# An mLSTM cell followed by a leaky-ReLU block: w_in in eight pieces, and the first chunk's mask and decay summed in PSUM

## The chip, the cores and the metric

The kernel runs on one core of a Trainium2 chip. The metric is the time of one execution on the device in microseconds. A core has TensorE (PE, matrix products into PSUM), VectorE (DVE), ScalarE (ACT), GpSimd (POOL) and SyncE (SP), which here issues DMAs. Each engine works through its own queue of instructions, and semaphores make one wait for another.

## The reference

Inputs are q, k, v and o_gate of shape (4, 8, 768, 40), two gates of shape (4, 8, 768), w_in (320, 2048) and w_out (2048, 320). Cut to what matters:

```python
for t in range(S):                       # S = 768, for each batch and head
    m_new = maximum(f[t] + m, i[t])
    fs, is_ = exp(f[t] + m - m_new), exp(i[t] - m_new)
    C = fs * C + is_ * outer(v[t], k[t])
    n = fs * n + is_ * k[t]
    den = maximum(abs(n @ q[t]), 1.0)
    y[t] = sigmoid(o[t]) * (C @ q[t]) / den
x = y as (B * S, H * D)                  # (3072, 320)
h = x @ w_in
out = maximum(0.01 * h, h) @ w_out       # (3072, 320)
```

The two weights arrive as 64-bit floats and are narrowed to 32 bits on the chip.

## The kernel before

The sequence is cut into six chunks of 128 positions. A "step" s is one chunk c and one batch b (s = 4c + b), with all eight heads. Within a chunk the recurrence is written as products: the decay between two positions is the exponential of a + bias, with a from scans along the sequence (`gates`, L193) and a triangular mask; the scores k.q are multiplied by it and then by v; the state C carries over what lies before the chunk.

For a step the units are these. `u_transpose` (L305) transposes k and q on PE into PSUM (tkq), and ACT copies them to SBUF (kqT, L314). `u_scores` (L316) makes the scores (sc, L323) and DVE multiplies the decay w by them (L327). `u_state` makes pc and dC (L337, L348), and in chunk 0 DVE copies dC into the state (L354). `u_values` multiplies w and v (pa, L367); in chunk 0 DVE copies pa to hn (L371) and makes den from it (L374 to L376). `gate` (L385, L388) makes x on DVE and POOL. `u_x` (L399 to L403) transposes x for the block that follows.

The decay w comes in two ways. From chunk 1 on, SP stores a in DRAM (L211) and reads it back spread over the partitions (`spread`, L255), POOL adds the mask (`prep_mask`, L279), and ACT takes the exponential (`prep_exp`, L287). In chunk 0, `spread_first` (L257) builds a spread over the partitions on PE (ab, L266), for two steps at a time, and DVE adds the mask (L273).

The feed-forward work of a chunk is `ff_units`. A first layer unit is, for chunk 0, a half: `half(j, h)` makes the features 2j and 2j + 1 for half h of the chunk's 512 rows (four products of L413 and two of L419, each of which is two instructions of 256 columns in the profile), and ACT applies the Prelu (L427). The second layer is `part(n, m)`, a quarter of the features for one block of 128 rows (L457), four parts to one output (L462).

Weights come in four pieces of w_in (four features each) and four of w_out. `load_weights(n)` issues the DMAs of piece n on SP into a raw 64-bit buffer, of which there are three. `narrow_weights(n)` (L154) is a generator that is called between other units: its first call queues the Abs on ACT (L166) and a first operation on DVE (L168), and each further call queues one more operation on DVE (L172, L176, L178, L180, L184). A piece may be used by PE after the sixth.

The order on PE, DVE, ACT and POOL is that of the code (a manual schedule); a scheduler orders SP. `first_chunk` (L503) writes out the order for chunk 0 by hand and puts in two halves, `ffs[0]` and `ffs[1]`, both from piece 0. The halves of a pair of j come together: (0, 1) for rows h = 0, then (0, 1) for h = 1, then (2, 3). The loop from L593 on takes the other thirty units of chunk 0's feed-forward work, with the cells of chunk 1 spread between them from unit 10 on; `todo` (L591) says at which unit the narrowing of a piece begins. Later chunks follow in the same way.

Of the kernel before, what the change touches and what calls it, by code (L numbers as in the profile page):

```python
# [9 lines left out]
F32 = mybir.dt.float32  # L10
# [8 lines left out]
def kernel(  # L19
# [90 lines left out]

    QN = NF // 4
    QC = 4 * P
    WC = KF * QC + 2 * P
    w_in = consts.tile([P, QN, WC], F32, name="w_in")
    w_out = consts.tile([P, NF, Dm], F32, name="w_out")

    def w_full(kk, f):
        n, e = divmod(f, 4)  # L120
        return w_in[:, n, kk * QC + e * P : kk * QC + (e + 1) * P]

    def w_rest(r, j):
        n, e = divmod(j, 2)
        return w_in[KR * r : KR * (r + 1), n, KF * QC + e * P : KF * QC + (e + 1) * P]

    wide = moe_w_in.dtype == U64
    raws = {}

    def load_weights(n):  # L130

        if n < QN:
            dst = w_in[:, n, :]
        else:
            dst = w_out[:, 4 * (n - QN) : 4 * (n - QN + 1), :].rearrange("p a d -> p (a d)")
        to = dst
        if wide:
            raw = wk.tile([P, dst.shape[1]], U64, name="raw", bufs=3)
            raws[n] = (raw, dst)
            to = raw[:]  # L140
        if n < QN:
            cols = slice(n * QC, (n + 1) * QC)
            for kk in range(KF):
                nc.sync.dma_start(to[:, ts(kk, QC)], moe_w_in[ts(kk, P), cols])
            rest = moe_w_in[KF * P :, cols].rearrange("d (j two e) -> two d j e", two=2, e=P)
            for r in range(2):
                nc.sync.dma_start(
                    to[KR * r : KR * (r + 1), KF * QC :].rearrange("p (j e) -> p j e", e=P), rest[r],
                )
        else:  # L150
            rows = moe_w_out[(n - QN) * QC : (n - QN + 1) * QC, :]
            nc.sync.dma_start(to.rearrange("p (a d) -> p a d", d=Dm), rows.rearrange("(a p) d -> p a d", p=P))

    def narrow_weights(n):  # L154
# [99 lines left out]
        d["w"] = wk.tile([P, H, P], F32, name="w", bufs=NL)  # L254
        nc.sync.dma_start(d["w"][:], a_dr[c, b * H : (b + 1) * H, :].partition_broadcast(P))  # L255

    def spread_first(a, s2):  # L257


        ab = [psf.tile([P, 2, H // RG, P], F32, name=f"ab{r}", tag="mm") for r in range(RG)]  # L260
        for n in range(2):
            for m in range(H // RG):
                for r in range(RG):
                    bh = (s2 + n) * H + m * RG + r
                    rows = ts(r, BH)
                    nc.tensor.matmul(  # L266
                        ab[r][:, n, m, :], lhsT=ident[rows, r * BH + bh : r * BH + bh + 1].to_broadcast([BH, P]),
                        rhs=a[rows, :], start=True, stop=True,
                    )
        for n in range(2):  # L270
            w = st[s2 + n]["w"] = wk.tile([P, H, P], F32, name="w", bufs=NL)
            for r in range(RG):
                nc.vector.tensor_tensor(  # L273
                    w[:, r::RG, :], ab[r][:, n], cmask[:].unsqueeze(1).to_broadcast([P, H // RG, P]), op=ALU.add,
                )

    def prep_mask(s):
        w = st[s]["w"]
# [2 lines left out]
    def prep_exp(s):  # L281

        c, b = divmod(s, B)
        w = st[s]["w"]
        for h in range(H):
            bh = b * H + h
            nc.scalar.activation(w[:, h, :], w[:, h, :], AF.Exp, bias=gT[:, c, 0, bh : bh + 1], scale=1.0)  # L287

    def prep_vu(s):

# [9 lines left out]
    def prep_o(s):  # L300

        nc.scalar.activation(st[s]["o"][:], st[s]["o"][:], AF.Tanh, scale=0.5)


    def u_transpose(s):  # L305
        d = st[s]
        d["kqT"] = wk.tile([P, 2, PR, P], F32, name="kqT")
        for i in range(2):
            tp = psc.tile([P, PR, P], F32, name="tkq", tag="c")
            for j in range(PR):  # L310
                nc.tensor.transpose(  # L311
                    tp[:, j, :], d["kq"][:, i, 2 * j : 2 * j + 2, :].rearrange("p h d -> p (h d)"), ident[:],
                )
            nc.scalar.copy(d["kqT"][:, i], tp[:])  # L314

    def u_scores(s):  # L316
        d = st[s]
# [11 lines left out]
    def u_state(s):  # L329
# [14 lines left out]
        if c + 1 < NB:  # L344
# [6 lines left out]
            for r in range(2):  # L351
                rows = slice(DP * r, DP * r + DP)
                if c == 0:
                    nc.vector.tensor_copy(C_new[rows, b, :, r, :], dC[rows])  # L354
                else:
                    g = gL[rows, c, b * H + r : (b + 1) * H : 2].unsqueeze(2).to_broadcast([DP, PR, D1])
                    nc.gpsimd.tensor_tensor(C_new[rows, b, :, r, :], C[rows, b, :, r, :], g, op=ALU.mult)
                    nc.vector.tensor_tensor(C_new[rows, b, :, r, :], C_new[rows, b, :, r, :], dC[rows], op=ALU.add)

    def u_values(s):  # L360
        c, b = divmod(s, B)
        d = st[s]
        hn = d["hn"] if c > 0 else wk.tile([P, H, D1], F32, name="hn")
        d["hn"] = hn
        pa = psc.tile([P, H, D1], F32, name="pa", tag="c")
        for h in range(H):
            nc.tensor.matmul(pa[:, h, :], lhsT=d["w"][:, h, :], rhs=d["va"][:, h, :], start=True, stop=True)  # L367
        if c > 0:
            nc.vector.tensor_tensor(hn[:], hn[:], pa[:], op=ALU.add)  # L369
        else:  # L370
            nc.vector.tensor_copy(hn[:], pa[:])  # L371

        den = d["den"] = wk.tile([P, H], F32, name="den")
        nc.vector.tensor_scalar(den[:], hn[:, :, D], scalar1=-2.0, scalar2=2.0, op0=ALU.mult, op1=ALU.max)  # L374
        nc.vector.scalar_tensor_tensor(den[:], in0=hn[:, :, D], scalar=2.0, in1=den[:], op0=ALU.mult, op1=ALU.max)
        nc.vector.reciprocal(den[:], den[:])  # L376
        if c > 0:
            gate(s)
# [28 lines left out]
    def ff_units(g):  # L407
# [56 lines left out]

        if g == 0:

            ins = [(j, h) for j0 in range(0, NF // 2, 2) for h in range(2) for j in (j0, j0 + 1)]
            return [lambda j=j, h=h: half(j, h) for j, h in ins] + [
                lambda n=n, m=m: part(n, m) for m in range(4) for n in range(B)
            ]  # L470
        return [u for j in range(NF // 2) for u in pair(j)] + [
# [26 lines left out]
    def feed(s):  # L498
        load(s)
        spread(s)  # L500
        load_o(s)

    def first_chunk():  # L503

        load(0)
        load(1)
        load_weights(0)
        load_o(0)
        load_o(1)
        load(2)  # L510
        load(3)
        load_weights(1)
        load_o(2)
        load_o(3)
        load_weights(2)
        load_weights(3)
        bu, a = gates(0)
        gates_T(0, bu)
        spread_first(a, 0)
        u_transpose(0)  # L520
        prep_exp(0)
        spread_first(a, 2)
        prep_vu(0)
        u_scores(0)
        u_state(0)
        prep_exp(1)
        u_transpose(1)
        prep_vu(1)
        bus[1] = gates(1)
        w = narrow_weights(0)  # L530
        next(w, None)
        next(w, None)
        u_values(0)
        prep_exp(2)
        u_scores(1)
        next(w, None)
        u_state(1)
        next(w, None)
        next(w, None)
        prep_o(0)  # L540
        u_values(1)
        gate(0)
        next(w, None)
        prep_o(1)
        gate(1)
        u_transpose(2)
        prep_vu(2)
        u_x(0)
        prep_exp(3)
        u_scores(2)  # L550
        u_x(1)
        u_state(2)
        ffs = ff_units(0)
        ffs[0]()
        u_transpose(3)
        prep_vu(3)
        w = narrow_weights(1)
        next(w, None)
        ffs[1]()
        next(w, None)  # L560
        prep_o(2)
        u_values(2)
        u_scores(3)
        gate(2)
        u_state(3)
        next(w, None)
        next(w, None)
        prep_o(3)
        u_values(3)
        gate(3)  # L570
        next(w, None)
        next(w, None)
        u_x(2)
        u_x(3)
        return ffs

    E = mybir.EngineType
    with tc.manual_schedule(engines={E.PE, E.DVE, E.Activation, E.Pool}):
        ffs = first_chunk()
        feed(B)  # L580
        load_weights(QN)
        load_weights(QN + 1)
        feed(B + 1)
        load_weights(QN + 2)
        load_weights(QN + 3)
        feed(B + 2)
        feed(B + 3)


        ffs = ffs[4:6] + ffs[2:4] + ffs[6:]  # L590
        todo = {0: 2, 4: 3, **{9 + 4 * n: QN + n for n in range(4)}}  # L591
        now = iter(())
        for c in range(1, NB + 1):  # L593
            if c > 1:
                ffs = ff_units(c - 1)
            cells = cell_units(c) if c < NB else []
            n_ff, n_c = len(ffs), len(cells)
            lead = 10 if c == 1 else 0
            done = 0
            for i in range(n_ff):  # L600
                if c == 1:
                    if i in todo:
                        for _ in now:
                            pass
                        now = narrow_weights(todo[i])
                    next(now, None)
                    next(now, None)
                    if i == 8:
                        u_gates(1)
                        ahead(B)  # L610
                if i == lead and c + 1 < NB:
                    bus[c + 1] = gates(c + 1)
                ffs[i]()
# [40 lines left out]
```

## Time and profile before

| | us |
|---|---|
| median of three runs | 622.41 (622.02 to 622.71) |
| the profiled execution | 623.18 |
| its span, first to last instruction | 621.0 |
| PE busy | 597.4 |
| PE idle by its timeline up to 165 us, the longest gaps | 5.5 (start), 2.9 at 30, 5.0 at 53, 1.7 at 93, 2.5 at 153 |
| four groups of DMA for one k, q or v tile, issue to landing | 3.1, 3.5, 2.8 (k, q, v) |
| w_in, 512 KB, issue to landing | 5.5 |

The page gives each engine's busy time, then the span in 40 slices of 15.5 us in tenths. In a timeline a line is start, duration, engine, source line, operation, operands and the number of instructions merged, and in brackets how long the engine had been idle and what ended that. In a table by stage the columns are the stage, its length, busy time of PE, of PE's weight loads, of DVE, ACT and POOL (with instructions), then the granted clock of TensorE, the busy share of the DMA engines and GB/s. Matrix products are pipelined: their rate is read from the distance between starts.

### The profile page before, as it was taken

What the parts mean: (1) busy time and instruction counts of PE and PEld (TensorE: products, weight loads), DVE (VectorE), ACT (ScalarE), POOL (GpSimd) and SP (SyncE); (2) the same over time, 40 slices, a digit from 0 to 9 for tenths busy, and PEclk for the clock granted to TensorE, in tenths of its full rate; (3) what the DMA queues carried; (4) which work ended last, traced back from release to release, by engine and by line L of the source; (5) the groups of instructions that cost most, each with busy time, mean ns of one, the idle gap of its engine ahead of it and who ended that gap; (6) DMA issues with size and microseconds to landing.
All of it is one profiled execution on the core that took longest, in us unless ns stands there. A gap on an engine that the chain in (4) does not pass through costs nothing.

```text
span 621.0 us, 7722 instructions
## 1 busy us (share of the span) xinstructions
PE 597.4 (96%) x3046; PEld 385.7 (62%) x3046; DVE 178.2 (29%) x343; ACT 185.7 (30%) x493; POOL 111.8 (18%) x110
## 2 busy tenths in 40 slices
PE   6986998998999999999999999999999999999997
PEld 5865666776554577654577745577745567743575
DVE  5838656886221121311121411211101111100000
ACT  4442345332334403144403144223043231012100
POOL 3023021554202220302202302202101010000000
PEclk9997999999899999999999999999999999999999
DMA  9999434433221331312321313303300000000000
GB/s 180 226 234 217 147 97 130 91 73 67 67 51 36 76 77 28 81 23 65 77 51 48 78 24 74 77 13 86 77 11 1 1 0 22 11 12 0 0 22 21
DMA packets 111346, 41.50 MB, mean 67 GB/s; under 512 B 101104, under 2 KB 105616, under 8 KB 111312
## 3 DMA queue, kind: packets, MB, share of 16 engines
q1 hardware_dynamic: 111024, 40.79, 29.0%
q8 instruction: 24, 0.39, 0.3%
q10 hardware_dynamic: 288, 0.23, 0.2%
q14 instruction: 10, 0.08, 0.0%
HBM read 37.00 MB, written 4.01 MB: 66 GB/s over the span
## 4 chain that ended last, share of the span: by engine, by line
PE 87%; DVE 5%; SPq 3%; POOL 1%; ACT 1%; issue 1%; DMA 1%; POOLq 0%; DVEq 0%; ACTq 0%
PE po L457 32%; PE ph L413 27%; PE ph L419 8%; PE pa L367 6%; PE sc L323 4%; PE pc L337 3%; PE tkq L311 3%; SPq L242 2%; PE dC L348 2%; POOL x L388 1%; PE xt L399 1%; DMA va<-in_v_dram 1%; DVE hn L369 1%; DVE x L385 1%; DVE w_in L176 0%
## 5 line engine op out<-in xcount | busy, mean ns | idle before, releaser
L457 PE MATMUL po<-w_out,act 128*128 128x320 f32 x768 | 221.4, 440 | 0.0
L413 PE MATMUL ph<-xT,w_in 128*128 128x512 f32 (+1 forms) x448 | 186.2, 552 | 0.4 <-DVE w_in L184 0.4
L457 PEld LDWEIGHTS po<-w_out,act 128*128 128x128 f32 x768 | 142.3, 191 | 55.0 <-issue 1.9
L413 PEld LDWEIGHTS ph<-xT,w_in 128*128 128x128 f32 x448 | 81.5, 195 | 68.8 <-issue 58.5
L427 ACT ACTIVATE act<-ph 128x512 f32<-128x512 f32 (+1 forms) x112 | 53.7, 531 | 151.6 <-PE ph L419 151.6
L388 POOL TENSOR_TENSOR x<-x,den 128x320 f32<-128x320 f32 x24 | 22.9, 955 | 396.6 <-DVE x L385 396.6
L327 DVE TENSOR_TENSOR w<-w,sc 128x512 f32<-128x512 f32 x48 | 30.7, 681 | 182.3 <-PE sc L323 182.3
L287 ACT ACTIVATE w<-w,gT 128x128 f32<-128x128 f32 x192 | 58.7, 397 | 13.0 <-POOL w L279 12.8
L419 PE MATMUL ph<-xT,w_in 64*128 64x512 f32 (+1 forms) x224 | 57.2, 588 | 0.0
L462 ACT COPY y<-po 128x320 f32<-128x320 f32 x24 | 10.2, 424 | 148.5 <-PE po L457 86.6
L367 PEld LDWEIGHTS pa<-va,w 128*128 128x128 f32 x384 | 49.1, 203 | 8.5 <-issue 5.9
L279 POOL TENSOR_TENSOR w<-w,cmask 128x1024 f32<-128x1024 f32 x20 | 50.1, 2503 | 0.0
L367 PE MATMUL pa<-va,w 128*128 128x41 f32 x384 | 49.5, 291 | 0.4 <-DVE w L327 0.4
L314 ACT COPY kqT<-tkq 128x512 f32<-128x512 f32 x48 | 26.1, 593 | 75.2 <-PE tkq L311 75.1
L419 PEld LDWEIGHTS ph<-xT,w_in 64*128 64x128 f32 x224 | 17.3, 189 | 36.3 <-issue 36.3
L323 PEld LDWEIGHTS sc<-kqT 40*128 40x128 f32 x384 | 26.1, 204 | 12.8 <-issue 5.3
L323 PE MATMUL sc<-kqT 40*128 40x128 f32 x384 | 30.4, 302 | 1.7 <-ACT kqT L314 1.7
L369 DVE TENSOR_TENSOR hn<-hn,pa 128x328 f32<-128x328 f32 x20 | 9.9, 496 | 74.9 <-PE pa L367 74.9
L311 PEld LDWEIGHTS tkq<-ident,kq 128*128 128x128 f32 x192 | 23.7, 152 | 10.8 <-issue 9.4
L311 PE MATMUL tkq<-ident,kq 128*128 128x128 f32 x192 | 28.3, 295 | 0.0
L341 DVE TENSOR_TENSOR hn<-pc,gT 128x328 f32<-128x328 f32 x20 | 10.0, 498 | 60.6 <-PE pc L337 60.6
L337 PEld LDWEIGHTS pc<-C,kqT 128*128 128x128 f32 x160 | 20.6, 191 | 7.0 <-issue 5.3
(65 smaller groups left out, 316.8 us busy)
## 6 DMA issues: line engine op xcount, KB each, us to landing
w<-a_dr SPq DMA_DIRECT2D x20, 512.0 KB, 4.9
raw<-in_moe_w_out_dram SPq DMA_DIRECT2D x4, 1280.0 KB, 5.7
raw<-in_moe_w_in_dram SPq DMA_DIRECT2D x8, 512.0 KB, 5.5
kq<-in_k_dram SPq DMA_DIRECT2D x24, 160.0 KB, 3.1
kq<-in_q_dram SPq DMA_DIRECT2D x24, 160.0 KB, 3.5
va<-in_v_dram SPq DMA_DIRECT2D x24, 160.0 KB, 2.8
o_sb<-in_o_gate_dram SPq DMA_DIRECT2D x24, 160.0 KB, 4.7
out_dram<-y SPq DMA_DIRECT2D x24, 160.0 KB, 1.8
```

Source lines behind the costliest of these rows:

```text
L279: nc.gpsimd.tensor_tensor(w[:], w[:], cmask[:].unsqueeze(1).to_broadcast([P, H, P]), op=ALU.add)
L287: nc.scalar.activation(w[:, h, :], w[:, h, :], AF.Exp, bias=gT[:, c, 0, bh : bh + 1], scale=1.0)
L311: nc.tensor.transpose(tp[:, j, :], d["kq"][:, i, 2 * j : 2 * j + 2, :].rearrange("p h d -> p (h d)"), ident[:],)
L323: nc.tensor.matmul(sc[r][:, j, :], lhsT=kqT[rows, 0, j, :], rhs=kqT[rows, 1, j, :], start=True, stop=True,)
L327: nc.vector.tensor_tensor(w[:, r::2, :], w[:, r::2, :], sc[r][:], op=ALU.mult)
L337: nc.tensor.matmul(pc[:, 2 * j : 2 * j + 2, :].rearrange("p h d -> p (h d)"), lhsT=d["kqT"][:, 1, j, :], rhs=C[:, b, j].rearrange("p h d - ...
L367: nc.tensor.matmul(pa[:, h, :], lhsT=d["w"][:, h, :], rhs=d["va"][:, h, :], start=True, stop=True)
L388: nc.gpsimd.tensor_tensor(x3, x3, d["den"][:].unsqueeze(2).to_broadcast([P, H, D]), op=ALU.mult)
L413: nc.tensor.matmul(ph[:, cols], lhsT=w_full(kk, f), rhs=xT[:, kk, cols], start=(kk == 0), stop=False,)
L419: nc.tensor.matmul(ph[r][:, cols], lhsT=w_rest(r, j), rhs=xT[KR * r : KR * (r + 1), KF, cols], start=False, stop=True,)
L427: nc.scalar.activation(acts[f][:, cols], ph[r][:, cols], AF.Prelu, alpha=0.01)
L457: nc.tensor.matmul(po[n][:], lhsT=acts[f][:, ts(n, P)], rhs=w_out[:, f, :], start=(f == 0), stop=(f == NF - 1),)
```

## The change

It does the following things.

- w_in is laid out in eight pieces of two features' columns each (640 columns in SBUF where there were 1280), and w_out is loaded in eight pieces too. Six raw buffers of half the size take the place of three.
- The halves of chunk 0 come as all eight j for rows h = 0, then all eight for h = 1. Half n of the first group uses piece n. `first_chunk` now holds all eight halves of the first group, with the narrowing of the eight pieces and the cells of steps 2 and 3 between them.
- In chunk 0 the mask is put into PSUM by a product of the identity and the mask (`mask_first`), and a is added by the products of `spread_first`, which no longer start a sum. The exponential on ACT reads PSUM. Steps 0 and 1 share four banks; steps 2 and 3 have two banks each and are made later, after `ffs[0]` and `ffs[2]`.
- For steps 0 and 1 DVE copies kqT; in chunk 0 ACT copies dC into the state, and hn is no longer copied: den and gate read pa in PSUM.
- `gates(1)` is called after `first_chunk`, and the loop for the remaining 24 units has the cells from unit 6 on and the narrowing of w_out, three operations to a unit, from unit 4 on.

The core of the diff:

```diff
-    QN = NF // 4
-    QC = 4 * P
+    NP = NF // 2
+    PC = 2 * P
...
-            raw = wk.tile([P, dst.shape[1]], U64, name="raw", bufs=3)
+            raw = wk.tile([P, dst.shape[1]], U64, name="raw", bufs=6)
...
+    def mask_first(steps, groups):
+        per = H // len(groups)
+        ab = {r: psf.tile([P, len(steps), per, P], F32, name=f"ab{r}", tag="mm") for r in groups}
+        for r in groups:
+            nc.tensor.matmul(
+                ab[r][:].rearrange("p n m t -> p (n m) t"), lhsT=ident[:],
+                rhs=cmask[:].unsqueeze(1).to_broadcast([P, len(steps) * per, P]), start=True, stop=False,
+                skip_group_check=True,
+            )
+        return ab
...
-                        rhs=a[rows, :], start=True, stop=True,
+                        rhs=a[rows, :], start=False, stop=True, skip_group_check=True,
...
-                nc.vector.tensor_tensor(
-                    w[:, r::RG, :], ab[r][:, n], cmask[:].unsqueeze(1).to_broadcast([P, H // RG, P]), op=ALU.add,
-                )
...
+            nc.scalar.activation(w[:, h, :], w[:, h, :] if c > 0 else st[s]["ab"][h], AF.Exp, bias=gT[:, c, 0, bh : bh + 1], scale=1.0)
...
+            if s < 2:
+                nc.vector.tensor_copy(d["kqT"][:, i], tp[:])
...
-                    nc.vector.tensor_copy(C_new[rows, b, :, r, :], dC[rows])
+                    nc.scalar.copy(C_new[rows, b, :, r, :], dC[rows])
...
-            ins = [(j, h) for j0 in range(0, NF // 2, 2) for h in range(2) for j in (j0, j0 + 1)]
-            return [lambda j=j, h=h: half(j, h) for j, h in ins] + [
+            return [lambda j=j, h=h: half(j, h) for h in range(2) for j in range(NP)] + [
...
+    narrowing = (x for n in range(2 * NP) for x in narrow_weights(n))
+    def narrow(count):
+        for _ in range(count):
+            next(narrowing, None)
...
+        ab = mask_first((0, 1), (0, 1, 2, 3))
         bu, a = gates(0)
         gates_T(0, bu)
+        spread_first(a, ab, (0, 1))
+        prep_exp(0)
         u_transpose(0)
...
+        narrow(3)
+        u_x(0)
+        u_x(1)
+        ffs = ff_units(0)
+        ffs[0]()
+        narrow(6)
+        ab = mask_first((2,), (0, 2))
+        spread_first(a, ab, (2,))
+        ffs[1]()
+        prep_exp(2)
+        narrow(6)
+        ffs[2]()
+        narrow(6)
+        ab = mask_first((3,), (0, 2))
+        spread_first(a, ab, (3,))
+        ffs[3]()
+        prep_exp(3)
+        narrow(6)
         u_transpose(2)
         prep_vu(2)
+        ffs[4]()
         u_scores(2)
+        narrow(3)
         u_state(2)
+        narrow(3)
+        u_values(2)
+        ffs[5]()
+        prep_o(2)
+        narrow(3)
+        gate(2)
         u_transpose(3)
         prep_vu(3)
+        narrow(3)
+        u_x(2)
         u_scores(3)
+        ffs[6]()
+        narrow(3)
         u_state(3)
+        u_values(3)
         prep_o(3)
         gate(3)
+        narrow(3)
+        ffs[7]()
         u_x(3)
-        return ffs
+        return ffs[8:]
...
+        bus[1] = gates(1)
...
-            lead = 10 if c == 1 else 0
+            lead = 6 if c == 1 else 0
...
+                if c == 1 and i >= 4:
+                    narrow(3)
+                if c == 1 and i == 5:
+                    u_gates(1)
+                    ahead(B)
```

## The prediction

> **What bounds the kernel now.** I read the page first, then the slices, then the table by stage, then the queues' timelines between 38 and 64 us.
>
> ```profile
> PE 597.4 (96%) x3046; PEld 385.7 (62%) x3046; DVE 178.2 (29%) x343; ACT 185.7 (30%) x493; POOL 111.8 (18%) x110
> PE   6986998998999999999999999999999999999997
> PEclk9997999999899999999999999999999999999999
> ```
>
> TensorE is busy 96%; the slices that are not full lie in the first sixth. Only there can a change of order gain or lose; from 165 us on PE is busy 451.8 of 456.0 us. The table by stage:
>
> ```profile
> 0.00:38.00 38.00, 29.40 (x227) 26.10 (x227) 25.30 (x60) 18.64 (x52) 8.97 (x20) 1.00 1.08 215
> 38.00:60.00 22.00, 16.21 (x106) 12.32 (x105) 12.62 (x22) 6.60 (x17) 4.76 (x3) 0.85 1.02 194
> 60.00:77.00 17.00, 17.00 (x73) 11.37 (x73) 10.56 (x10) 5.85 (x14) 1.34 (x1) 0.90 0.57 184
> ```
>
> "Busy" hides the clock. PE's timeline:
>
> ```profile
> 38.02 3.78 PE L413 MATMUL ph<-xT,w_in 128*128 128x256 f32 x8
> 41.73 1.23 PE L419 MATMUL ph<-xT,w_in 64*128 64x256 f32 x4
> ...
> 43.84 1.89 PE L413 MATMUL ph<-xT,w_in 128*128 128x256 f32 x8
> 45.66 0.70 PE L419 MATMUL ph<-xT,w_in 64*128 64x256 f32 x4
> ...
> 57.83 0.69 PE L399 MATMUL xt<-ident,x 128*128 128x128 f32 x2 [4.98 <-POOL x L388]
> 58.31 0.42 PE L400 MATMUL xt<-ident,x 128*64 128x128 f32 x1
> 59.18 3.35 PE L413 MATMUL ph<-xT,w_in 128*128 128x256 f32 x7 [0.45 <-DVE w_in L184]
> ```
>
> The same half (eight L413, four L419) takes 4.94 us at 38.02 and 2.56 at 43.84: PE runs at half rate up to about 43 us, where the clock column still reads 1.00 (no record yet), and again after the gap of 4.98. The two queues that feed PE:
>
> ```profile
> 42.99 0.66 ACT L427 ACTIVATE act<-ph 128x256 f32<-128x256 f32 x2 [4.75 <-PE ph L419]
> 43.66 1.07 ACT L314 COPY kqT<-tkq 128x512 f32<-128x512 f32 x2
> 44.62 1.39 ACT L166 ACTIVATE w_in<-raw 128x1280 f32<-128x1280 f32 x1
> ```
>
> ```profile
> 46.04 0.83 DVE L168 TENSOR_SCALAR wm<-w_in 128x1280 f32<-128x1280 f32 x1 [7.24 <-ACT w_in L166]
> 46.90 0.83 DVE L172 TENSOR_SCALAR wm<-wm 128x1280 uint32<-128x1280 uint32 x1
> ```
>
> ACT's Abs, the first step of narrowing a piece, stands behind the Prelu of the half before it, and DVE waits 7.24 us for that Abs. In this kernel it costs PE nothing: a piece of w_in serves four halves.
>
> **What the Trainium skill says.** "TensorE: Matmul & The Clock Gate", Part 1: the clock starts at half rate, is released after a window of about 3.4 us of sustained work and taken back after an idle one. The trace agrees: 3.4 us of dense L413 from 38.0 on preceded the doubling, the 4.98 gap undid it. The trace adds that the busy but thin work of 8 to 30 us (41-column products, 32- and 40-row products) never released it. Same page, "Architectural detail": ScalarE and VectorE are strict FIFO, only TensorE pulls weight loads ahead. The trace agrees: the 7.24 us above. "PSUM — Partial Sum Buffer", rule 2: a first matmul clears a bank's has-written bits and the following ones add; that is what lets mask and a be summed in a bank. No row of before shows this.
>
> **The change, part by part.** Times are positions in the profiled span. My mark is the moment when eight halves and all cells of chunk 0 are done. In before two halves were done by 46.4; the timeline has the next starting at 59.18, 63.85, 66.41, 68.97, 71.52 and 74.08 and the one after them at 76.64, so the mark is 76.6.
>
> *Masks.* Four products of 512 columns, two instructions each. L413 with 256 columns goes every 0.427 us at half clock, so 8 x 0.853 = 6.8 us from about 1.7 (cmask is written at 1.65). tg started at 5.51, so it is late by 1.4 (if the clock is released on the way) to 3.1 us; I take 8.0 for the end. In return it is the first dense block of 3.4 us, so I expect full clock from 5 to 8.6 us on.
>
> *Cells 0 and 1.* Removed from the path: 16 adds of L273 (5.5 us DVE), the hn copies (4 x 0.50), C copies (8 x 0.32, to ACT); added: four kqT copies on DVE of about 0.69 (from hn's 0.50 at 328 columns and L327's 0.64 at 512). DVE waits in this stage, so the net 7.3 us saved counts nothing by itself; without that cover it would be a gain of as much. PE at full clock: tg 0.5, ab 1.2, twice 1.12 + 1.16 + 0.67 + 1.92 = 9.7, some 3.5 of waits on DVE (kqT, the product with the scores; pa is now held until its gate has read it): 8.0 + 14.9 = 23. Then den, gate, POOL (0.7 to 1.9), xt, xT: 5. The first half starts at 28; at half clock throughout at 34 or so. I take 29 (38.0 before).
>
> *The halves.* Half n+1 needs piece n+1. In the compiled order ACT has Prelu n, then Abs n+1, then Prelu n+1. So: half n on PE, Prelu 0.66, Abs, six DVE steps, half n+1, and nothing overlaps. Abs of 640: half of 1.37 is 0.69, with a fixed part 0.8; I take 0.75. DVE: 0.83 and 1.49 at 1280 columns, 0.17 at 8 columns, so 0.50 and 0.83; three each, 4.0 us (half of the old 7.1 is 3.6, with the 0.03 pitches 4.2). Handovers of 0.03 to 0.05: 0.1. One link without the half: 5.5 us. Added by what stands in the same queues: Exp of step 2 and of step 3 on ACT (2.45 each, links 1-2 and 3-4); in link 4-5 the scores and their DVE product (7.1 in all); in 5-6 Tanh, gate, POOL, xt, scores (7.9); in 6-7 den and gate (6.6). Sum of links: 5.5 + 8.0 + 5.5 + 8.0 + 7.1 + 7.9 + 6.6 + 0.7 (last xt) = 49.3.
>
> The gaps of PE are 3 to 8 us long; 4.98 and 2.45 (at 152.7, then 24 po in 8.15 for 6.46) both cost the clock. Halves 0, 2, 4, 7 start cold and take about 4.7, half 6 about 4.2; halves 1, 3, 5 follow masks or cell work and take 2.55: 30.7. End: 29 + 49.3 + 30.7 = 109, against 76.6: **+32.4 us**.
>
> *Masks and a of steps 2 and 3* (4 x 0.86 and 2 x 0.86 warm) lie in gaps of PE: nothing; in a full queue 5.2 us.
>
> *SP.* The loads of w_in come in pieces of 640 KB, four DMAs each (32 for 16), most of them ahead of the k, q, v of steps 2 and 3, which are first used in link 3-4, some 70 us in; they are issued by about 35: hidden. Raw buffers are six half-size ones; loads of pieces 6 and 7 wait for pieces 0 and 1, five links ahead of use, landing takes 5.5: hidden; a late piece would cost its lateness once. The store of a and the spreads move behind them and behind gates(1), from 29.8 to about 105; 3.4 + 6.2 us to land, first used five halves (12.8 us) later: hidden; if not, the excess.
>
> *After the mark* the second half group runs densely. DVE and ACT are tighter there: gT waits behind a whole w_out piece, then Exp, Abs, three DVE steps, gates(2), Prelu, kqT before the first scores. Before had a gap of 1.66 here; I get 4.0 and a possible clock loss of 1.7, so +2.3 to +4.0, taken 3.0. The gap of 2.45 at the end stays.
>
> Sum +35.4: the span of 621.0 becomes 656.4, the profiled execution's 623.2 becomes 658.6 (2.2 lie outside the span). The median 622.4 is 0.8 below that execution: **658**.
>
> **The rivals.** (B) The clock stays up: all eight halves 2.55 (20.4), start 28: 97.7, +21.1, and +2.3 later: 646. For it: 46 to 50 us was thin and stayed warm; against: the gaps of 2.45 and 4.98. (C) The masks don't hold the clock and all is cold: start 34, halves 38.8, sum 122, +46, and +4: 672. (D) Faster: Abs n+1 runs ahead of Prelu n, so that DVE alone sets the pace. Then piece n is done at 25 + 4n, and cells 2 and 3 are what comes late: I get 71.6 for the mark, -5.0, and +2.3: 619.7. It decides if Abs 1 starts before half 0 ends; only ACT's queue order speaks, and it speaks against it. That the masks do not arrive in the sum would show in the output, not in time.
>
> **How the numbers follow.** Likeliest (serial links, mixed clock) 0.57; B 0.22; C 0.17; D 0.03; no change 0.01. 0.2% is about what a measurement here can tell from no change. Range 644 to 672: from B's price with 3.6 us pieces to C. Slower 0.96, same 0.01, faster 0.03.
>
> **What would show it.** Abs 1 on ACT starts right after the Prelu of half 0, and DVE's first step of each piece waits for ACT; PE waits for DVE before halves 1 to 7, some 5.5 to 8 us; clock at 0.5 in many of these stages; the stage from 165 on unchanged but shifted. Wrong if Abs runs ahead, if halves follow at 4 us, or if the first half starts later than 34.

## The result, and the profile after

| | before | after |
|---|---|---|
| median of 4 runs each, us | 622.21 (621.29 to 622.71) | 666.23 (665.28 to 668.5) |
| ratio | | 1.0715 (95% interval 1.0683 to 1.0746) |
| profiled execution and its span, us | 623.18; 621.0 | 665.66; 663.6 |
| the mark (eight halves and all cells of chunk 0 done), us | 76.64 (76.57 in PE's timeline) | 106.81 |

The kernel became slower by 44 us, against a forecast of 35.6. (The two medians above give a ratio of 1.0707; 1.0715 fits the 621.8 us that the kernel before takes in the runs of the experiments below.) The page of the kernel after, its first rows and the granted clock:

```profile
PE 612.6 (92%) x3062; PEld 389.5 (59%) x3062; DVE 177.5 (27%) x367; ACT 184.6 (28%) x505; POOL 101.7 (15%) x110
PE   8745768798979999999999999999999999999997
PEclk9678778987999999999999999999999999999999
```

DVE and ACT have as much to do as before, POOL less; nobody is overloaded. The first seven slices (116 us) are thinly filled, and the clock column, which was nearly all 9, has 6, 7 and 8 there. PE's own busy time rose by 15 us. The 16 new mask instructions took 10.2 of it (5.91, 2.23 and 2.02 us by the timeline); the other 5 go with more time at half clock: up to 200 us, and counting the start up to the first release, 71 us against 57 by the clock's records. The table by stage has the same columns as before:

```profile
0.00:24.71 24.71, 18.99 (x163) 13.22 (x164) 14.29 (x34) 10.07 (x32) 7.10 (x18) 0.90 0.92 198
24.71:65.00 40.29, 23.90 (x96) 14.77 (x96) 13.41 (x21) 10.52 (x31) 0.73 (x1) 0.75 0.72 151
65.00:106.80 41.80, 27.88 (x158) 20.63 (x158) 20.91 (x40) 8.57 (x24) 2.90 (x3) 0.72 0.38 100
106.80:200.00 93.20, 82.55 (x480) 61.98 (x481) 57.10 (x101) 32.69 (x94) 26.79 (x23) 0.91 0.32 81
200.00:663.60 463.60, 459.25 (x2167) 278.93 (x2165) 71.83 (x173) 122.78 (x327) 64.16 (x66) 1.00 0.17 40
```

From 24.71 to 106.8 us PE is busy 51.8 of 82.1 us, and DVE (34.3) and ACT (19.1) idle for more than half of it too: that is what a chain looks like, in which mostly one engine works at a time. After 200 us all is as before. PE's timeline shows the chain from its end; the releaser in brackets is DVE's last operation on the next piece:

```profile
24.71 3.75 PE L423 MATMUL ph<-xT,w_in 128*128 128x256 f32 x8 [0.73 <-DVE w_in L182]
28.39 1.23 PE L429 MATMUL ph<-xT,w_in 64*128 64x256 f32 x4
29.55 2.23 PE L260 MATMUL ab<-cmask,ident 128*128 128x512 f32 x4
31.71 1.16 PE L276 MATMUL ab<-a,ident 32*128 32x128 f32 x16
35.30 1.97 PE L423 MATMUL ph<-xT,w_in 128*128 128x256 f32 x8 [2.43 <-DVE w_in L182]
37.19 0.70 PE L429 MATMUL ph<-xT,w_in 64*128 64x256 f32 x4
45.62 3.75 PE L423 MATMUL ph<-xT,w_in 128*128 128x256 f32 x8 [7.73 <-DVE w_in L182]
```

ACT and DVE between these halves, in order of their queues:

```profile
29.65 0.66 ACT L437 ACTIVATE act<-ph 128x256 f32<-128x256 f32 x2 [4.82 <-PE ph L429]
30.20 0.79 ACT L164 ACTIVATE w_in<-raw 128x640 f32<-128x640 f32 x1
37.92 0.66 ACT L437 ACTIVATE act<-ph 128x256 f32<-128x256 f32 x2 [6.93 <-PE ph L429]
38.47 2.18 ACT L294 ACTIVATE w<-ab,gT 128x128 f32<-128x128 f32 x8
40.47 0.84 ACT L164 ACTIVATE w_in<-raw 128x640 f32<-128x640 f32 x1
```

```profile
31.02 0.49 DVE L166 TENSOR_SCALAR wm<-w_in 128x640 f32<-128x640 f32 x1 [6.46 <-ACT w_in L164]
...
34.32 0.82 DVE L182 TENSOR_TENSOR w_in<-w_in,wm 128x640 f32<-128x640 f32 x1
41.34 0.49 DVE L166 TENSOR_SCALAR wm<-w_in 128x640 f32<-128x640 f32 x1 [6.20 <-ACT w_in L164]
```

Half 0 ends on PE, Prelu at 29.65, Abs at 30.20 straight after it, DVE from 31.02 to 35.14, half 1 at 35.30. In the next link Exp (2.18 us) stands ahead of Abs as well. The waits of the whole execution, summed (total, times, longest), first PE's in the kernel before:

```profile
PE ph L413 <- DVE w_in L184: 0.4, 1, 0.4
```

and then in the kernel after:

```profile
PE ph L423 <- DVE w_in L182: 26.1, 7, 7.7
DVE wm L166 <- ACT w_in L164: 37.5, 7, 7.3
DVE wm L166 <- ACT w_out L164: 27.8, 6, 15.7
```

After the mark, PE has three gaps that are new or longer than before, and two stretches of half clock with the first two of them. First the counterpart of the first gap in the kernel before, then the three:

```profile
94.99 1.23 PE L323 MATMUL sc<-kqT 40*128 40x128 f32 x16 [1.66 <-ACT kqT L314]
```

```profile
132.61 1.72 PE L333 MATMUL sc<-kqT 40*128 40x128 f32 x12 [3.92 <-ACT kqT L324]
156.96 2.50 PE L467 MATMUL po<-w_out,act 128*128 128x320 f32 x4 [2.48 <-DVE w_out L182]
193.76 1.34 PE L467 MATMUL po<-w_out,act 128*128 128x320 f32 x4 [1.47 <-DVE w_out L182]
```

The clock's records are at half from 132.5 to 139.3 and from 156.4 to 166.6.

### The profile page after: what moved, and what is told of

It reads as the page before. It is cut to its first block, busy times and chain, and to the rows that moved or that the text cites. A ratio compares the mean times of both kernels' runs of the same rounds, so it can differ in the third digit from the quotient of the medians.

```text
span 663.6 us, 7844 instructions
## 1 busy us (share of the span) xinstructions
PE 612.6 (92%) x3062; PEld 389.5 (59%) x3062; DVE 177.5 (27%) x367; ACT 184.6 (28%) x505; POOL 101.7 (15%) x110
## 4 chain that ended last, share of the span: by engine, by line
PE 79%; DVE 11%; ACT 5%; SPq 2%; issue 1%; POOL 1%; DMA 1%; POOLq 0%; DVEq 0%; ACTq 0%
PE po L467 28%; PE ph L423 27%; PE ph L429 8%; PE pa L377 5%; PE sc L333 3%; PE tkq L318 2%; PE pc L347 2%; ACT w L294 2%; DVE wm L178 2%; PE dC L358 1%; DVE wm L170 1%; DVE w_out L174 1%; DVE wm L166 1%; DVE w_in L174 1%; DVE w_in L182 1%
## 5 line engine op out<-in xcount | busy, mean ns | idle before, releaser
L467 PE MATMUL po<-w_out,act 128*128 128x320 f32 x768 | 225.8, 445 | 3.9 <-DVE w_out L182 3.9
L423 PE MATMUL ph<-xT,w_in 128*128 128x512 f32 (+1 forms) x448 | 193.5, 572 | 26.7 <-DVE w_in L182 26.1
L467 PEld LDWEIGHTS po<-w_out,act 128*128 128x128 f32 x768 | 143.8, 194 | 60.8 <-DVE w_out L182 5.0
L423 PEld LDWEIGHTS ph<-xT,w_in 128*128 128x128 f32 x448 | 86.1, 205 | 96.5 <-issue 77.7
L398 POOL TENSOR_TENSOR x<-x,den 128x320 f32<-128x320 f32 x24 | 18.6, 773 | 442.9 <-DVE x L395 442.9
L294 ACT ACTIVATE w<-w,gT 128x128 f32<-128x128 f32 x160 | 49.0, 399 | 10.4 <-POOL w L284 7.2
L472 ACT COPY y<-po 128x320 f32<-128x320 f32 x24 | 10.2, 424 | 147.0 <-PE po L467 85.1
L284 POOL TENSOR_TENSOR w<-w,cmask 128x1024 f32<-128x1024 f32 x20 | 48.5, 2425 | 8.7 <-DMA w<-a_dr 8.7
L324 ACT COPY kqT<-tkq 128x512 f32<-128x512 f32 x44 | 23.7, 597 | 78.7 <-PE tkq L318 78.7
L318 PEld LDWEIGHTS tkq<-ident,kq 128*128 128x128 f32 x192 | 21.9, 143 | 11.3 <-issue 9.7
L318 PE MATMUL tkq<-ident,kq 128*128 128x128 f32 x192 | 26.0, 279 | 0.0
```

Of the source, the lines that this page charges most:

```text
L284: nc.gpsimd.tensor_tensor(w[:], w[:], cmask[:].unsqueeze(1).to_broadcast([P, H, P]), op=ALU.add)
L294: nc.scalar.activation(w[:, h, :], w[:, h, :] if c > 0 else st[s]["ab"][h], AF.Exp, bias=gT[:, c, 0, bh : bh + 1], scale=1.0)
L318: nc.tensor.transpose(tp[:, j, :], d["kq"][:, i, 2 * j : 2 * j + 2, :].rearrange("p h d -> p (h d)"), ident[:],)
L423: nc.tensor.matmul(ph[:, cols], lhsT=w_full(kk, f), rhs=xT[:, kk, cols], start=(kk == 0), stop=False,)
L467: nc.tensor.matmul(po[n][:], lhsT=acts[f][:, ts(n, P)], rhs=w_out[:, f, :], start=(f == 0), stop=(f == NF - 1),)
```

## The experiments

The theory after the result: (1) in the link ACT's queue order (Prelu n ahead of Abs n+1) makes the eight pieces serial; (2) the gaps that this makes cost clock on top; (3) the part after the mark comes from w_out's narrowing, which stands in the same queues and starts late. The rivals were that DVE's own pace or the cells set the links whatever the order, that idle clock is a by-product worth little, and that the new way of making the masks is itself what costs. The table gives the time, the ratio to the kernel before from runs on the same chip (there it takes 621.8), the start of the first half and the mark, from the profiled execution. In the experiments line numbers differ from those of the kernel after by the lines that an edit adds. The first half and the mark come from one execution each: chunk 0 is the same code in the kernel after and in the run with w_out early, and their marks differ by 2.1 us. The execution of the kernel before (623.18) lies 1.4 above its median of 621.8, so its mark is probably late by about as much.

| run | us | ratio to before | first half | mark | span after the mark |
|---|---|---|---|---|---|
| before | 621.8 | 1 | 38.02 | 76.64 | 544.4 |
| after | 666.23 | 1.0715 [1.0683, 1.0746] | 24.71 | 106.81 | 556.8 |
| Abs one piece ahead | 641.48 | 1.0308 [1.0288, 1.0328] | 24.80 | 82.52 | 557.3 |
| gaps filled | 653.08 | 1.0496 [1.0477, 1.0515] | 25.46 | 94.39 | 556.0 |
| masks alone | 621.31 | 0.9984 [0.9977, 0.9991] | 38.39 | 74.96 | 544.4 |
| w_out early | 656.14 | 1.0544 [1.0525, 1.0563] | 24.49 | 108.90 | 546.9 |
| reordered | 617.12 | 0.9922 [0.9907, 0.9937] | 25.87 | 71.67 | 544.6 |
| reordered and filled | 614.54 | 0.9882 [0.9865, 0.9898] | 26.17 | 69.39 | 543.9 |

**Abs one piece ahead.** ACT's Abs of piece n+1 is queued when the narrowing of piece n begins, so ahead of the Prelu of half n; all else is the kernel after.

```diff
-        nc.scalar.activation(dst, hi.bitcast(F32), AF.Abs)
+        if n == 0 or n >= NP:
+            nc.scalar.activation(dst, hi.bitcast(F32), AF.Abs)
+        if n + 1 < NP:
+            raw1, dst1 = raws[n + 1]
+            hi1 = raw1[:].bitcast(U32).rearrange("p (c two) -> p c two", two=2)[:, :, 1]
+            nc.scalar.activation(dst1, hi1.bitcast(F32), AF.Abs)
```

> The changed kernel with one edit: ACT's Abs of w_in piece n+1 is queued when the narrowing of piece n begins, so ahead of the Prelu of half n. Queue-order theory (the loop half, Prelu, Abs, six DVE operations, half is serial because of the place of Abs in ACT's queue): the waits of DVE for Abs of 5 to 7 us before pieces 1 to 4 go, pieces follow at about 4 us, the eight halves and the cells of chunk 0 are done at 71 to 77 us instead of 106.8, and the time falls from 666 to 631 to 637. Clock theory (the loss lies in TensorE running at half rate, the order only triggers it): the halves stay at 4 to 5 us, and at most 10 to 15 us come back: 650 to 656.

Measured: 641.48 us, 24.7 less than the kernel after, and the mark 24.3 earlier at 82.5. PE's timeline for the same three halves, and the longest gap that is left:

```profile
24.80 3.75 PE L428 MATMUL ph<-xT,w_in 128*128 128x256 f32 x8 [0.72 <-DVE w_in L187]
...
32.83 1.99 PE L428 MATMUL ph<-xT,w_in 128*128 128x256 f32 x8
...
35.92 1.99 PE L428 MATMUL ph<-xT,w_in 128*128 128x256 f32 x8 [0.47 <-ACT act L442]
...
76.71 3.78 PE L428 MATMUL ph<-xT,w_in 128*128 128x256 f32 x8 [3.64 <-DVE w_in L187]
```

The gaps of 2.43 and 7.73 are gone or 0.47. So the order is what made the links, and DVE's work (4.1 us a piece) is not. The miss is in the size: this theory had 631 to 637 us and a mark of 71 to 77. What is left: DVE still waits for Abs 2.29 and 3.66 us behind Exp, the gate of step 2 waits 3.81 us for a Tanh queued behind a Prelu, den of step 3 waits 2.31 us for PE with a piece's remaining steps queued behind it, and PE was at half clock for 30.7 us between 20 and 81 us. One piece of lead is too short where ACT also has an Exp to do. The loss after the mark stays (557.3 us against 544.4).

**Gaps filled.** 31 idle products of 512 columns, to a PSUM tile that nobody reads, stand in PE's queue where the kernel after had its gaps; nothing is moved.

```diff
+    def fill(count):
+        junk = psf.tile([P, 4, P], F32, name="junk", tag="mm")
+        for _ in range(count):
+            nc.tensor.matmul(
+                junk[:].rearrange("p n t -> p (n t)"), lhsT=ident[:],
+                rhs=cmask[:].unsqueeze(1).to_broadcast([P, 4, P]), start=True, stop=True, skip_group_check=True,
+            )
...
+        fill(8)
         ffs[2]()
```

> The changed kernel with idle products put into PE's gaps before halves 0 to 7 (31 products of the identity and the mask, 0.86 us each at full clock, into a bank nobody reads), so that the clock has no reason to fall. Queue-order theory: the links between halves keep their 5.5 us and more; only the halves fall, from 33.3 us in all to about 20.5, so 10 to 13 us come back: 653 to 656. Clock theory: most of the 44 us come back: 625 to 635.

Measured: 653.08 us, 13.1 less. From the first release (6.7) up to the mark the clock is at half only from 20.3 to 23.7, and all eight halves go at full rate (starts to ends 2.6 us). The waits of this kernel:

```profile
DVE wm L166 <- ACT w_in L164: 28.8, 7, 6.2
DVE wm L166 <- ACT w_out L164: 28.2, 6, 13.9
PE ph L423 <- DVE w_in L182: 4.2, 5, 1.6
```

DVE waits for Abs as often as in the kernel after, seven times: the links are still serial. PE's own wait is short because idle products fill it. The chain's mark moves from 106.8 to 94.4. So the clock is worth about 12.4 us of the mark's 30.2, on top of a chain that remains (two profiled executions, and the idle products delay the first half by 0.75 us). That the clock alone makes the loss is ruled out: with the clock up, 31 us are left of 44.

**Masks alone.** In the kernel before, with its four pieces and its order of halves, the mask and a of chunk 0 are summed in PSUM as in the kernel after, with kqT on DVE and dC on ACT. `gates(1)` and the steps of the first narrowing are moved as well.

```diff
+        ab = mask_first((0, 1), (0, 1, 2, 3))
         bu, a = gates(0)
         gates_T(0, bu)
-        spread_first(a, 0)
+        spread_first(a, ab, (0, 1))
+        prep_exp(0)
         u_transpose(0)
-        prep_exp(0)
-        spread_first(a, 2)
...
-        bus[1] = gates(1)
         w = narrow_weights(0)
...
+        for s in (2, 3):
+            ab = mask_first((s,), (0, 2))
+            spread_first(a, ab, (s,))
+        bus[1] = gates(1)
+        prep_exp(2)
         u_transpose(2)
```

> The kernel before with the other part of the change alone: mask and a of chunk 0 summed in PSUM, Exp from PSUM, kqT of steps 0 and 1 on DVE, dC copies on ACT, no hn copy; w_in stays in four pieces, with two halves in the first chunk. Theory that the masks pay (they release the clock at 5 to 8 us and take DVE adds off the path): the first half starts at 25 to 28 us instead of 38.0, and 5 to 11 us are gained: 611 to 617. Rival (the 6 us of mask products only delay the first transposes, and what is gained is waited for at piece 1 of w_in): 620 to 625.

Measured: 621.31 us, ratio 0.9984, so a gain of 0.5 us that the interval keeps apart from nothing. The rival (this part alone is about neutral) holds; my theory's early first half (25 to 28 us) does not: it starts at 38.39. PE and ACT of this kernel show where the time went:

```profile
14.42 1.98 PE L379 MATMUL pa<-va,w 128*128 128x41 f32 x16
16.33 1.16 PE L335 MATMUL sc<-kqT 40*128 40x128 f32 x16
17.42 1.01 PE L360 MATMUL dC<-vu,kq 128*64 128x41 f32 x16
18.36 3.78 PE L379 MATMUL pa<-va,w 128*128 128x41 f32 x16
21.94 3.76 PE L262 MATMUL ab<-cmask,ident 128*128 128x512 f32 x4
25.63 2.08 PE L278 MATMUL ab<-a,ident 32*128 32x128 f32 x16
27.64 3.73 PE L262 MATMUL ab<-cmask,ident 128*128 128x512 f32 x4
```

```profile
31.48 0.40 ACT L214 ACTIVATE bu<-bu,a 32x128 f32<-32x128 f32 x1 [10.31 <-DVE bu L213]
31.79 0.29 ACT L215 ACTIVATE bu<-a 32x128 f32<-32x128 f32 x1
32.09 2.18 ACT L296 ACTIVATE w<-ab,gT 128x128 f32<-128x128 f32 x8
```

The clock fell at 17.5 us, in the 41-column products; the mask products of steps 2 and 3 then took 3.7 us each at half clock, and ACT waited 10.31 us for `gates(1)`, which stood on DVE behind the first piece. That order is my edit's, so this run is one arrangement of the masks and no bound on what they can give.

**w_out early.** The kernel after, with the narrowing of w_out from unit 0 of the loop instead of unit 4 and its Abs one piece ahead.

```diff
-        nc.scalar.activation(dst, hi.bitcast(F32), AF.Abs)
+        if n <= NP:
+            nc.scalar.activation(dst, hi.bitcast(F32), AF.Abs)
+        if NP <= n < 2 * NP - 1:
+            raw1, dst1 = raws[n + 1]
+            hi1 = raw1[:].bitcast(U32).rearrange("p (c two) -> p c two", two=2)[:, :, 1]
+            nc.scalar.activation(dst1, hi1.bitcast(F32), AF.Abs)
...
-                if c == 1 and i >= 4:
+                if c == 1:
                     narrow(3)
```

> The changed kernel with w_out alone treated otherwise: its narrowing begins at unit 0 of the loop instead of unit 4, and ACT's Abs of each of its pieces is queued one piece ahead. w_in and chunk 0 as in the changed kernel. Theory that the 12.4 us lost after the first half group come from w_out's place in the queues (the gap of 3.9 us before the first scores of chunk 1, waits of 2.5 and 1.5 us for pieces, and 17 us at half clock behind them): the first half group still ends at 106 to 107 us, and 8 to 11 us come back: 655 to 658. Rival (the gap before the scores comes from gates(2) ahead of the kqT copies in ACT's queue, as the gap of 1.7 us in the kernel before, and the rest from DVE being full): 2 to 4 us come back: 662 to 664.

Measured: 656.14 us, 10.1 less than the kernel after. The part after the mark is 546.9 us, 2.5 more than before; in the kernel after it was 12.4 more. Both gaps at po are gone, and so are the 10.2 us of half clock that followed the first. The run makes two moves, the earlier start and the earlier Abs, and doesn't tell which of them did it. Its mark, 108.90, lies past the 106 to 107 that was expected, though chunk 0 is unchanged. The gap at the first scores remains:

```profile
134.38 1.27 PE L338 MATMUL sc<-kqT 40*128 40x128 f32 x16 [3.12 <-ACT kqT L329]
```

ACT has there `bu` of `gates(2)` (2.73 us of waiting for DVE), a Prelu and then kqT. That gap was in the forecast; the po gaps were not.

**Reordered.** All the orders that these runs named, together: Abs two pieces ahead for w_in and w_out, Tanh of steps 2 and 3 earlier, the gate of step 2 ahead of a piece's remaining DVE steps, piece 7's remaining steps ahead of den and gate of step 3, w_out from unit 0.

```diff
+    def abs_of(n):
+        if wide and n < 2 * NP:
+            raw, dst = raws[n]
+            hi = raw[:].bitcast(U32).rearrange("p (c two) -> p c two", two=2)[:, :, 1]
+            nc.scalar.activation(dst, hi.bitcast(F32), AF.Abs)
...
+        abs_of(0)
+        abs_of(1)
         narrow(2)
...
+        abs_of(2)
         ffs[0]()
...
+        prep_o(2)
+        abs_of(5)
         ffs[3]()
...
+        prep_o(3)
+        abs_of(7)
         ffs[5]()
-        prep_o(2)
+        gate(2)
         narrow(3)
-        gate(2)
...
+        narrow(3)
         u_values(3)
-        prep_o(3)
         gate(3)
-        narrow(3)
+        abs_of(9)
         ffs[7]()
```

> The change with its queues put in another order: Abs of w_in and w_out two pieces ahead of their use, each ahead of the Prelu of the half before; Tanh of steps 2 and 3 ahead of the halves, den and gate of step 3 behind the last DVE operation of piece 7, w_out from unit 0 on. Theory that order in the queues is the whole cause: DVE sets the pace with 4 us a piece, the first half group ends at 66 to 73 us (76.6 in the kernel before), nothing is lost later, and the time is 610 to 618, under both kernels. Rival (eight small pieces with their DVE work between the halves cost by themselves, through gaps and the clock that falls in them): 622 to 632.

Measured: 617.12 us, 49.1 less than the kernel after and 0.78% less than the kernel before. The mark is at 71.67, the longest gap of PE ahead of a half is 1.01 us, and 544.6 us follow the mark, as before the change:

```profile
55.62 3.46 PE L429 MATMUL ph<-xT,w_in 128*128 128x256 f32 x8 [1.01 <-DVE w_in L188]
...
71.67 1.99 PE L429 MATMUL ph<-xT,w_in 128*128 128x256 f32 x8 [0.53 <-ACT xT L417]
```

The same instructions in another order (PE 3062, DVE 367 and ACT 505 on the pages of both): the loss was order. Which of the moves are needed beside the Abs was not tried one by one.

**Reordered and filled.** The kernel above with three idle products between the values of step 1 and the first half.

```diff
+        fill(2)
         u_x(0)
         u_x(1)
+        fill(1)
         ffs = ff_units(0)
```

> As e6_reordered, with three idle products of the identity and the mask in PE's gaps between the last values of step 1 and the first half, to hold the clock there. If the clock falls at about 20 us in e6_reordered as it did in the changed kernel, the first half takes 2.6 instead of 4.9 us here, and with the products after it 3 to 4 us are gained on PE; where DVE sets the pace less of it counts: 0 to 4 us under e6_reordered. If the clock is not what the first half waits for: the same or up to 1 us more.

Measured: 614.54 us, 2.6 below the reordered kernel and 1.18% below the kernel before (ratio 0.9882 [0.9865, 0.9898]). PE at the first half and the mark:

```profile
20.04 3.76 PE L529 MATMUL junk<-cmask,ident 128*128 128x512 f32 x4
...
26.17 1.89 PE L429 MATMUL ph<-xT,w_in 128*128 128x256 f32 x8
...
69.39 1.99 PE L429 MATMUL ph<-xT,w_in 128*128 128x256 f32 x8 [0.53 <-ACT xT L417]
```

The first half starts 0.3 us later than without the fill and takes half as long; the mark comes 2.3 us earlier. It is the best version measured here.

## Why the prediction was right, and where its sum was off

The direction, the mechanism and the range (644 to 672) held; the single time was 8.2 us short. Part of that is luck. The mark came within 2.2 us because a first half that was 4.3 us early made up for halves that took 2.6 more, and the step after the mark missed by 9.4 us, which the range covered only with the room that it had up to C (672), and C did not happen. By the prediction's own steps, in the profiled execution:

| step | forecast | measured | shown by |
|---|---|---|---|
| masks end | 8.0 us | 7.6 | timeline; tg at 7.54 |
| first half starts | 29 | 24.71 | timeline |
| eight halves | 30.7 | 33.3 | lengths 4.84, 2.59, 4.84, 3.68, 4.10, 4.05, 4.86, 4.38, each to the end of its last product or the start of what follows it |
| links | 49.3 | 48.8 | 106.81 - 24.71 - 33.3 |
| mark against before | +32.4 | +30.2 | timelines |
| after the mark | +3.0 | +12.4 | (663.6 - 106.81) - (621.0 - 76.64) |
| sum | +35.4 | +42.6 | spans 663.6 and 621.0 |

*The links.* The mechanism was as forecast: Abs follows the Prelu of the half before it, and nothing overlaps. In link 0-1 the pieces of the sum were 0.55 from the Prelu to the Abs, 0.79 for the Abs (forecast 0.75), 4.12 for DVE's six operations (4.0), and 5.65 from Prelu to half 1 (5.5). That ACT's order was the cause is shown by the run with Abs ahead. The links' sum came within 0.5 us, and the single links, from the end of one half to the start of the next, came within 0.7: 5.75, 7.73, 5.73, 7.79, 6.47, 7.44, 6.78 and 1.07 for 5.5, 8.0, 5.5, 8.0, 7.1, 7.9, 6.6 and 0.7. Of the signs that were named, DVE's first step waits for ACT on every piece but piece 5. PE's waits for DVE are 2.28 to 7.73 us where 5.5 to 8 were named, because masks and cells fill part of each link; half 6 has none, since there POOL's x ended the gap (4.03 us).

*The first half* came 4.3 us earlier. The values of step 1 end at 20.3, where I had 23 (masks 8.0 and 14.9 for the cells), and den to xT took 4.4, where I had 5 and rounded up by 1. The clock was released at 6.2 as forecast, but it was taken back at 19.84, which I had not forecast; that is why half 0 is cold. The prediction read two things of this kind wrong in the kernel before. There the clock came up at 42.98, after 5.0 us of the first half and not 3.4. It fell at 53.2, only 0.4 us into the gap of 4.98, so that gap as a whole did not undo it; the thin work just ahead of it is the nearer cause, as the last section argues. The half at 43.84 took 2.52 us by its lines, not 2.56.

*The halves* took 2.6 more. I had counted 1, 3 and 5 as warm; halves 3 and 5 ran in part at half clock (3.68 and 4.05). The run with filled gaps puts a price on the clock as a whole: 12.4 us of the mark.

*The masks and a of steps 2 and 3* lay in gaps and cost nothing, as forecast: PE waited for DVE at 35.30 whatever it did at 29.55. The masks alone, in the other order of halves, were worth +0.5 us of gain.

*SP.* None of PE's gaps before a half was put down to a DMA; the releasers are DVE and POOL. The loads were hidden, as forecast.

*After the mark* is the step that was mis-sized: "taken 3.0", measured 12.4. The gap at the first scores was right (4.0 forecast, 3.92 measured) and so was the one of 2.45 that stays. Left out was w_out's narrowing as a supplier of PE: it starts at unit 4 of the loop, DVE waits 27.8 us for its Abs in six times (15.65 at 118.50, since no piece is begun before), and twice a piece of it comes late for po: 2.48 and 1.47 us. The gaps together are 10.3 against 5.1 us, so +5.3; the clock is at half for 17.1 us against 3.4, up to (17.1 - 3.4) / 2 = 6.8 us more. That makes up to 12.1 of 12.4, an estimate. The run with w_out early shows it: 12.4 became 2.5.

*The rivals.* B (clock up, 646) did not happen, but the filled kernel shows its world: mark at 94.4 where B had 97.7; with the 11.6 us after the mark that B hadn't either, 653. C (all cold) did not happen: the clock was up for 13.7 us of the first 20 and in parts of each later link. D (Abs ahead, 619.7) was rightly kept small, because the order of the kernel after is what the code says; made true by an edit, one piece of lead alone gives 641, and the whole order 617 with the mark at 71.67, where D had 71.6. So D's price belongs to the whole order, not to the one move that it named.

What stays open: how much of the 7.2 us by which the last kernel beats the one before comes from the masks in PSUM, and how much from the pieces and the order; no run has the pieces and the order without the masks.

## What to carry to other kernels

When a weight is cut into smaller pieces so that each feeds one unit of work, look at every in-order engine that both prepares piece n+1 and finishes unit n: if the preparation is queued behind the finishing, the pipeline is serial, and smaller pieces make it worse, because the old large piece covered several units (PE waited 0.4 us for narrowed w_in before, 26.1 after). Queue the first step of the next pieces ahead by as many units as the longest other job in that queue asks for. Here one piece of lead left 641 us and two, together with the other moves, gave 617; two alone was not tried. And follow the moved work to the end of its own list: here its tail, w_out, cost 10 us a good while after the stage that was changed.

## What the runs showed of the hardware

The clock was taken back while PE was busy. The Trainium skill, "TensorE: Matmul & The Clock Gate", "HAM oscillation", gives the rule to have no PE-idle gaps above about 3.4 us; this case is stricter. From 16.4 to 19.8 us in the kernel after PE is busy 87% of the time by its records, yet the clock fell at 19.84. The work there is 41-column products:

```profile
13.86 1.98 PE L377 MATMUL pa<-va,w 128*128 128x41 f32 x16
...
18.37 1.90 PE L377 MATMUL pa<-va,w 128*128 128x41 f32 x14 [0.18 <-DVE w L337]
```

They go every 0.12 us, and if a column costs what it costs in a 256-column product (0.216 us for 256 at full clock, 0.427 at half), 41 columns stream for 0.035 us of that at full clock. I counted each product so, overlapping ones once, over the stretches of 3.41 us that the clock's records mark out (their distances are multiples of it). The result is an estimate from these figures. The stretch before that fall streams 35% of its time; the two before it, which kept the clock, 52% each. Over the kernel after up to 177 us, each fall followed a stretch of 35% or less, and stretches of 41% and more kept the clock. In the kernel before, 49.8 to 53.2 us is busy 78%, streams 26%, and lost the clock. The gap of 2.48 us lost it at 156.4, in a stretch of 33%. Each release in the kernel after followed a stretch of 81% or more, but stretches of 89% (at 88.1) and 86% (at 132.5) were not followed by one.

The other runs blur the border. Counted in the same way, falls follow stretches of 46 and 48% in the run of the masks alone and of up to 52% in the reordered kernel (at 92.8), while in the run with Abs one piece ahead a stretch of 38% (at 149.5) kept the clock. In the masks alone PE is busy for 3.40 of the 3.41 us from 14.1 to 17.5, and the clock falls at 17.5. So "busy" in a profile did not foretell the clock, the sum of columns did only roughly, and no rule comes out of these executions.

A DVE step with two inputs on a piece took 0.82 us mostly, but 2.87, 2.87 and 2.86 in the kernel after (at 145.97, 165.97 and 181.87). Each time POOL's addition of a mask (L284) ran beside it, for 2.60 to 2.94 us, and DVE's step ended 0.7 us after it. That they hinder each other is what this suggests; no run tried it.

Exp of a step reads its sum from PSUM in 2.18 us for eight; from SBUF eight take 2.45 (148.19 in the same execution).
